# Two small tiles allocated elsewhere in a fused S4D and MLP kernel, so that every operand of the first MLP layer begins at the same place modulo 256 bytes

## The chip, the cores and the metric

The kernel runs on one core of a Trainium2 chip. The metric is the device time of one launch in microseconds (us). Times of engines come from one profiled execution, in which every instruction has a start and a duration. The engines are named as the profile names them: PE (TensorE, matmuls), PEld (TensorE's weight loads, which run beside its matmuls), DVE (VectorE), ACT (ScalarE), POOL (GpSimd) and SP (SyncE, which issues DMAs here).

## The reference

The input is `u`, 2048 tokens of 576 channels, in float32. It is normalised over the channels, and goes two ways that are multiplied at the end:

```python
x  = A_u
xn = _layernorm(x)
s  = A(xn)          # S4D: K = 2 Re sum_n C_n exp(A_n dt t); a causal convolution of each channel
                    # over 2048 tokens, by FFT of length 4096; + xn * D_skip
g  = silu(B(xn))    # MLP: gelu(layernorm(xn) @ w1 + b1) @ w2 + b2, 576 -> 4608 -> 576
out = x + s * g
```

## The kernel before

**The MLP sets the frame.** Tokens come in four blocks of 512 (two halves of the program, with `tb` = 0 and 1 in each), the 4608 hidden units in 12 groups of 384 = 3 x 128. One *slot* is one group for one block of 512 tokens; there are 4 x 12 = 48 slots. Each float32 operand is split into a high part and a low part of the type fp32r, and a product is made of three: high by high, high by low, low by high.

- Layer 1 (`layer1`, line 501; the first slot has its own version, `first_layer1`, line 515) makes three 128 x 512 results in a slot, each by 14 matmuls: four channel blocks of 128 three times, and two matmuls for the last 64 channels, which stand with their low parts in one tile of 128 rows. The stationary operand (loaded as weights) is a 128 x 128 piece of `w1h`, `w1l`, `w1r` or `w1s`; the moving operand is 512 columns of `XH`, `XL` or `XR`. In all there are 48 x 3 x 14 = 2016 of these matmuls.
- After each result `hidden` (line 537) has ACT make the gelu (`h32`) and its high part `hh`, and DVE the low part `hl`.
- Layer 2 (`layer2`, line 554) takes pieces of `hh` and `hl` as weights and 288 columns of `w2h` or `w2l` as the moving operand. The 576 output channels are two halves, `dh` = 0 and 1. Its last four calls of a slot are 9 matmuls each, all of one half: token block 2 with `dh` = 0, then `dh` = 1, then token block 3 with both. There are 3456 matmuls of this form. DVE adds each result to `acc`.

**The S4D part is laid between.** Tables of phases and magnitudes (DVE and ACT, tiles `w`, `mg`, `U`, `v`), the kernel K from them (`kgen`), and a two-stage FFT in matmuls of 32 rows or columns on the tile `A2`. Which of its steps stands where is decided when the program is built: the class `Order` keeps an estimated time for each engine and traces each step when its inputs are due, and pins the order. The order on each engine is thus fixed in the built program.

**Before all that** the prologue runs 22 matmuls on zeros (`warm_up`, line 1133; moving operand and weights are both the last block of `XL`), normalises the first four row blocks, splits the first `w1`, and transposes.

**Tiles.** A tile that is given out once takes the next free bytes of each SBUF partition, in the order of the calls `sb.tile`. So a tile's address follows from what was allocated ahead of it; a start is rounded up to 32 bytes or more. The tile `dsk` (576 bytes a partition, the skip weights) is allocated on line 399, after `XR`; the tile `st` (48 bytes, statistics of a norm) is allocated inside `stats` (line 365), so at its first call `na[0][0](0)` on line 1138, just ahead of `w1_tiles()`.

Of the kernel before, what the change touches and what calls it, by code (L numbers as in the profile page):

```python
# [9 lines left out]
F32 = mybir.dt.float32  # L10
# [7 lines left out]
L, D, N, F = 2048, 576, 128, 4608  # L18
P = 128
# [192 lines left out]
def mixer_kernel(ctx, tc, u, log_a_real, a_imag, c_real, c_imag, log_dt, d_skip, w1, b1, w2, b2,  # L212
                 f1, f2, g2, g1, tvals, ident, out, parts=("mlp", "s4d")):
    nc = tc.nc
    sb = ctx.enter_context(tc.tile_pool(name="sb", bufs=1))
# [13 lines left out]
    def tok(t, b, p0=0, n=P):  # L229
        return dram(t, (b + 16 * p0) * D, [[16 * D, n], [1, D]])  # L230
# [24 lines left out]
    tv, small = tvs[:, :NV], tvs[:, NV:]  # L255
    b1t = sb.tile([P, F // P], F32, name="b1t")
    halfpi, epst = small[:, 0:2], small[:, 2:4]
    w1s = sb.tile([P, G * P], F32R, name="w1s")

    def load_tv():  # L260
# [53 lines left out]
    nc.vector.memset(epst[:, 0:1], EPS)  # L314
    nc.vector.memset(epst[:, 1:2], EPS * EPS)
    nc.vector.memset(w1s[64:].bitcast(F32), 0.0)


    YT, XT = {}, {}
# [28 lines left out]
    def norms(b0, n):  # L348

        def stats(t, part=None):
            if part == 1:
                pass
            elif t == 0 and b0 in (1, 3):
                MV[b0] = SECOND.pop()
            elif t == 0:
                a, r = (UV[:, D + 8 * b0 + 8 * k:D + 8 * b0 + 8 * k + 8] for k in range(2))
                a, r = a.rearrange("p (t k) -> p t k", k=2), r.rearrange("p (k t) -> p k t", k=2)
                MV[b0] = a[:, :n], r[:, :, :n]  # L360
                if n == 1:
                    SECOND.append((a[:, 1:2], r[:, :, 1:2]))
                    PAIR[b0 + 1] = r[:, :, :2]
            if part != 1:
                MV["st"] = sb.tile([P, 2, 6], F32, name="st")
            st = MV["st"]
            for i in range(2) if part is None else (part,):
                nc.vector.bn_stats(st[:, i], XT[b0 + t][:, i * 288:(i + 1) * 288])
            if part != 0:
                nc.vector.bn_aggr(MV[b0][0][:, t], st)  # L370

        def roots():
            mv, rs = MV[b0]
            nc.scalar.activation(rs[:, 0], mv[:, :, 1], AF.Sqrt, bias=epst[:, 0:1], scale=1.0)
            nc.scalar.activation(rs[:, 1], mv[:, :, 1], AF.Sqrt, bias=epst[:, 1:2], scale=1.0 + EPS)

        def recip():
            nc.vector.reciprocal(MV[b0][1], MV[b0][1])

        def second(t):  # L380
            mv, rs = MV[b0]
            y = sb.tile([P, D], F32, name="row", bufs=NROW)
            nc.vector.tensor_scalar(y, XT[b0 + t], mv[:, t, 0:1], rs[:, 1, t:t + 1], op0=OP.subtract, op1=OP.mult)
            if b0 >= 8:
                nc.sync.dma_start(y_s[b0 + t - 8], y)
            else:
                YT[b0 + t] = y

        def first(t):
            mv, rs = MV[b0]  # L390
            x = XT.pop(b0 + t)
            nc.gpsimd.tensor_scalar(x, x, mv[:, t, 0:1], rs[:, 0, t:t + 1], op0=OP.subtract, op1=OP.mult)
            nc.gpsimd.dma_start(tok(xn_s, b0 + t), x)
        return stats, roots, recip, second, first
# [1 line left out]
    XH = sb.tile([P, KB, 2, TB], F32R, name="XH")  # L396
    XL = sb.tile([P, KB, 2, TB], F32R, name="XL")
    XR = sb.tile([P, 2, TB], F32R, name="XR")
    dsk = sb.tile([P, D // 4], F32, name="dsk")
    nc.vector.memset(dsk, 0.0)  # L400

    def y_load(b):
        y = sb.tile([P, D], F32, name="row", bufs=NROW)
# [59 lines left out]
    def w1_tiles():  # L463
        W[1] = (sb.tile([P, KB, G * P], F32R, name="w1h"), sb.tile([P, KB, G * P], F32R, name="w1l"),
                sb.tile([P, G * P], F32R, name="w1r"), w1s)
# [667 lines left out]
    def warm_up(n):  # L1133
        for _ in range(n):
            nc.tensor.matmul(qb[:, 0], zero[:, :P], zero, start=True, stop=True)
    warm_up(22)
    na = [norms(b, 1) for b in range(4)]
    na[0][0](0)
    w1_tiles()

    nc.gpsimd.tensor_copy(small[:, 4:5], MV[0][0][:, 0, 0:1])
    nc.gpsimd.dma_start(idp, dram(ident, 0, [[P, 64], [64 * P, 2], [1, P]]))
# [381 lines left out]
```

## Time and profile before

| | before |
|---|---|
| median of 3 runs | 1108.05 us (1106.91 to 1109.93) |
| the profiled execution, its own time | 1107.08 us |
| its span, first to last instruction | 1105.3 us |
| granted TensorE clock, mean | 0.999 |
| PE busy | 1088.8 us, 99% |
| PEld busy | 941.5 us, 85% |
| DVE busy | 940.9 us, 85% |
| ACT busy | 657.1 us, 59% |
| POOL busy | 197.9 us, 18% |

How it is read: a matmul's duration in a row is its way through the array, near 390 ns for 512 columns, and the next one begins long before it ends. So the pace of a stream of matmuls is read from start to start, not from durations. In the view of instructions in order of time a row has the start, the time from that start to the end of the last instruction in the row, the engine, the line, and behind an x how many instructions the row holds. A matmul's weights are loaded while the matmul before it runs.

### The profile page before, as it was taken

The numbers are of one execution on the slowest core, as the hardware profiler recorded it, in microseconds if no ns is written. First come the engines' busy times: TensorE is split into PE (matmuls) and PEld (weight loads), VectorE is DVE, ScalarE is ACT, GpSimd is POOL, SyncE is SP. The second block draws the span as 40 slices with busy tenths as digits, with TensorE's granted clock in tenths as the row PEclk, the third lists the DMA queues.
The fourth block names the chain that finished last, engine by engine and source line by source line (L and its number), as shares of the span: only waits on it lengthen the run. The fifth ranks groups of instructions, "written<-read, shape, count | busy, mean of one in ns | idle before, by whom it ended". The sixth has DMA issues, their size and how long they took to land.

```text
span 1105.3 us, 27245 instructions
## 1 busy us (share of the span) xinstructions
PE 1088.8 (99%) x11547; PEld 941.5 (85%) x11547; DVE 940.9 (85%) x1510; ACT 657.1 (59%) x977; POOL 197.9 (18%) x282
## 2 busy tenths in 40 slices
PE   9999999999999999999999999999999999999997
PEld 7889989888888888888888888888888888888896
DVE  7799698978999999989699998999999976666466
ACT  6666688666656556657866755665764733233333
POOL 5584532011000200010100001000100021110231
PEclk9999999999999999999999999999999999999999
DMA  8645557333233231633322322233412455342254
GB/s 244 224 147 182 192 205 209 103 107 114 65 87 83 72 93 40 140 94 99 106 85 89 69 77 78 67 98 49 125 22 95 109 139 179 87 127 83 60 186 114
DMA packets 111513, 125.54 MB, mean 114 GB/s; under 512 B 59940, under 2 KB 82032, under 8 KB 110368
## 3 DMA queue, kind: packets, MB, share of 16 engines
q1 hardware_dynamic: 95728, 76.44, 24.7%
q0 software_dynamic: 15104, 46.49, 13.6%
q8 instruction: 90, 1.47, 0.5%
q10 hardware_dynamic: 560, 0.89, 0.3%
q14 instruction: 31, 0.25, 0.1%
HBM read 95.52 MB, written 34.01 MB: 117 GB/s over the span
## 4 chain that ended last, share of the span: by engine, by line
PE 84%; DVE 11%; ACT 2%; issue 2%; DMA 1%; SPq 0%; DVEq 0%; ACTq 0%
PE mxb L569 19%; PE mxa L569 19%; PE mxa L512 19%; PE mxb L512 16%; PE cv L889 3%; PE cv L1000 3%; PE cv L1053 2%; PE cv L962 2%; DVE hl L551 1%; DVE w2l L489 1%; DVE acc L577 1%; PE cv L1080 1%; DVE mg L832 1%; DVE A L949 1%; DVE w L807 1%
## 5 line engine op out<-in xcount | busy, mean ns | idle before, releaser
L569 PE MATMUL mxa<-w2h,hl 128*128 128x288 f32 x573 | 170.0, 297 | 4.0 <-DVE hl L551 4.0
L569 PE MATMUL mxb<-w2h,hh 128*128 128x288 f32 x576 | 171.6, 298 | 0.0
L569 PE MATMUL mxa<-w2h,hh 128*128 128x288 f32 x573 | 171.0, 298 | 0.3 <-DVE acc L577 0.3
L569 PE MATMUL mxb<-w2h,hl 128*128 128x288 f32 x576 | 170.2, 296 | 0.0
L569 PE MATMUL mxb<-w2l,hh 128*128 128x288 f32 x576 | 169.5, 294 | 0.0
L569 PE MATMUL mxa<-w2l,hh 128*128 128x288 f32 x573 | 168.6, 294 | 0.0
L551 DVE TENSOR_TENSOR hl<-h,hh 128x512 fp32r<-128x512 f32 x144 | 98.7, 687 | 73.4 <-ACT hh L548 72.9
L789 POOL DMA_DIRECT2D par<-par_s x36 | 27.4, 761 | 533.0 <-DVE mg L832 520.1
L545 ACT ACTIVATE h<-mxa,b1t 128x512 f32<-128x512 f32 x73 | 50.0, 687 | 117.0 <-PE mxa L512 115.1
L569 PEld LDWEIGHTS mxb<-w2h,hh 128*128 128x128 f32 x576 | 108.1, 188 | 8.6 <-issue 2.9
L569 PEld LDWEIGHTS mxa<-w2h,hh 128*128 128x128 f32 x573 | 107.5, 188 | 7.9 <-issue 2.3
L569 PEld LDWEIGHTS mxa<-w2h,hl 128*128 128x128 f32 x573 | 107.6, 188 | 5.6 <-DVE hl L551 5.6
L569 PEld LDWEIGHTS mxb<-w2l,hh 128*128 128x128 f32 x576 | 108.2, 188 | 0.8
L569 PEld LDWEIGHTS mxa<-w2l,hh 128*128 128x128 f32 x573 | 107.7, 188 | 0.8
L569 PEld LDWEIGHTS mxb<-w2h,hl 128*128 128x128 f32 x576 | 108.1, 188 | 0.0
L545 ACT ACTIVATE h<-mxb,b1t 128x512 f32<-128x512 f32 x71 | 48.9, 688 | 91.3 <-PE mxb L512 90.3
L548 ACT ACTIVATE hh<-h 128x512 fp32r<-128x512 f32 x144 | 90.8, 631 | 4.2
L492 ACT ACTIVATE w2h<-raw 128x576 fp32r<-128x576 f32 x72 | 44.5, 675 | 63.2 <-PE mxa L569 63.1
L577 DVE TENSOR_TENSOR acc<-mxb,acc 128x576 f32<-128x576 f32 x88 | 65.8, 748 | 17.5 <-PE mxb L569 17.3
L512 PE MATMUL mxa<-XH,w1h 128*128 128x512 f32 x284 | 79.3, 400 | 0.5 <-DVE acc L577 0.5
L512 PE MATMUL mxb<-XH,w1h 128*128 128x512 f32 x280 | 78.7, 402 | 0.5 <-ACT h L545 0.5
L577 DVE TENSOR_TENSOR acc<-mxa,acc 128x576 f32<-128x576 f32 x88 | 65.4, 743 | 15.9 <-PE mxa L569 15.5
(235 smaller groups left out, 2483.6 us busy)
## 6 DMA issues: line engine op xcount, KB each, us to landing
raw<-in_B_w_dram SPq DMA_DIRECT2D x72, 288.0 KB, 3.2
raw<-in_B_w_dram SPq DMA_DIRECT2D x96, 192.0 KB, 2.9
par_s<-A POOLq DMA_DIRECT2D x8, 1080.0 KB, 4.8
par<-par_s POOLq DMA_DIRECT2D x36, 240.0 KB, 3.3
f2t<-f2q SPq DMA_DIRECT2D x24, 256.0 KB, 3.4
raw<-in_B_w_dram SPq DMA_DIRECT2D x48, 96.0 KB, 3.3
u_s<-in_A_u_dram POOLq DMA_DIRECT2D x16, 288.0 KB, 4.4
xc<-xn_s SPq DMA_DIRECT2D x48, 96.0 KB, 3.9
```

The source lines that it names most:

```text
L492: nc.scalar.activation(h, r, AF.Copy)
L512: nc.tensor.matmul(q, a, b, start=j == 0, stop=j == len(ops) - 1)
L545: nc.scalar.activation(t, q, AF.Gelu_apprx_tanh, bias=b1t[:, g * G + i:g * G + i + 1], scale=1.0)
L548: LAST[0] = nc.scalar.activation(hh[:, i], t, AF.Copy)
L551: nc.vector.tensor_sub(hl[:, i], t, hh[:, i].bitcast(F32))
L569: nc.tensor.matmul(q[:, dh, :288], a[:, i, c], b[:, i, d], start=i == 0 and k == 0, stop=i == G - 1 and k == 2)
L577: nc.vector.tensor_add(o, q[:, dh:dh + n, :288], b if g == 0 else o)
L789: nc.gpsimd.dma_start(PAR[b].rearrange("p (g i) k -> p g (i k)", g=4), dram(par_s, (b // 6 * CH + b % 6 * 4) * NPAR, [[D * NPAR, P], [24 * ...
L889: nc.tensor.matmul(q[32 * g:32 * g + 32, i // 2, i % 2 * 64:i % 2 * 64 + 64], U[:, ri, 4 * g + i, :], v[:, ri, 4 * g + i, :], start=ri == ...
L962: nc.tensor.matmul(Q1ST[i, x][g // 2][64 * f:64 * f + 64, g % 2].rearrange(order), f1t[r].rearrange("p s k -> p (s k)"), rhs(r, f), start= ...
L1000: nc.tensor.matmul(Q[i][32 * q:32 * q + 32, f, 2 * ri:2 * ri + 2], m[r, 4 * i + q, 32 * ri:32 * ri + 32], A2[r, 4 * p + 2 * i + q // 2, :, ...
L1053: nc.tensor.matmul(QI[q // 2][64 * f:64 * f + 64, q % 2, i], MAT["g2t", p + i // 2][r, i % 2, ri], YS[p + i // 2][0][r, i % 2, ri, f], sta ...
```

## The change

Three lines move. `dsk` is allocated ahead of `w1s`, its clearing stands with the other clearings of the prologue, and `w1_tiles()`, which only allocates, is called ahead of the first `stats`.

```diff
     b1t = sb.tile([P, F // P], F32, name="b1t")
     halfpi, epst = small[:, 0:2], small[:, 2:4]
+    dsk = sb.tile([P, D // 4], F32, name="dsk")
     w1s = sb.tile([P, G * P], F32R, name="w1s")
...
     nc.vector.memset(w1s[64:].bitcast(F32), 0.0)
+    nc.vector.memset(dsk, 0.0)
...
     XR = sb.tile([P, 2, TB], F32R, name="XR")
-    dsk = sb.tile([P, D // 4], F32, name="dsk")
-    nc.vector.memset(dsk, 0.0)
...
     na = [norms(b, 1) for b in range(4)]
+    w1_tiles()
     na[0][0](0)
-    w1_tiles()
```

In the built program every engine has the same instructions in the same order, with the same waits and the same semaphores. What differs is where tiles lie. Bytes from the start of a partition, and the rest modulo 256:

| tile | before | after |
|---|---|---|
| `XH`, `XL`, `XR` (moving, layer 1) | 74944, 91328, 107712: 192 | 75520, 91904, 108288: 0 |
| `w1h`, `w1l`, `w1r` (weights, layer 1) | 120128, 126272, 132416: 64 | 120064, 126208, 132352: 0 |
| `w1s` (weights, layer 1) | 26304: 192 | 26880: 0 |
| `A2`, `acc`, `U` | 27840, 52416, 70848: 192 | 28416, 52992, 71424: 0 |
| `dsk` | 111808: 192 | 26304: 192 |
| `st` | 120064: 0 | 133888: 0 |
| `raw` | 112384: 0 | the same |
| `h32`, `w2h`, `w2l`, `hh`, `hl`, `v`, `f2t`, `kt`, `xc` | 64 | the same |
| `bias2`, `f1t`, `g1t`, `idp` | 128 | the same |

The pieces that a matmul of layer 1 takes begin whole multiples of 512 bytes into their tiles, so they have the rest of the tile. In layer 2 the weights begin at 64; the moving pieces are 2304 = 9 x 256 bytes apart by hidden block and 1152 = 4.5 x 256 bytes by half, so that `dh` = 0 begins at 64 and `dh` = 1 at 192.

## The prediction

> **What bounds the kernel now.** I read the first part of the page, then its chain of work that ended last, then PE's waits, and then the instructions in order of time, since only there a pace can be read.
>
> ```profile
> span 1105.3 us, 27245 instructions
> PE 1088.8 (99%) x11547; PEld 941.5 (85%) x11547; DVE 940.9 (85%) x1510; ACT 657.1 (59%) x977; POOL 197.9 (18%) x282
> PE 84%; DVE 11%; ACT 2%; issue 2%; DMA 1%; SPq 0%; DVEq 0%; ACTq 0%
> ```
>
> PE is busy for 99% of the span, and 84% of the chain is PE itself (the third line), another 2% its own issue. The longest waits of its matmuls say the same:
>
> ```profile
> PE mxa L569 <- DVE hl L551: 4.0, 7, 1.2
> PE mxa L1135 <- POOL XL L1129: 1.3, 1, 1.3
> PE cv L1053 <- issue: 1.2, 1, 1.2
> ```
>
> Four microseconds in seven waits is the most that any one cause costs. So the time is the number of matmuls times their pace, and a change of pace is a change of time, but for the 13% of the chain that DVE and ACT hold. How near DVE is shows in a view by stretches (length; then busy time of PE, PEld, DVE, ACT and POOL, with the number of instructions in brackets; then clock, DMA share, GB/s):
>
> ```profile
> 35.00:300.00 265.00, 264.16 (x2100) 232.45 (x2099) 230.40 (x354) 183.65 (x246) 87.52 (x113) 1.00 0.47 152
> 600.00:900.00 300.00, 296.13 (x3918) 253.28 (x3917) 283.58 (x444) 187.97 (x275) 22.63 (x36) 1.00 0.32 82
> ```
>
> From 600 to 900 us DVE works 283.58 of 300 us: there it can follow a faster PE by some 5%, no more. The clock is 1.00 in both, so no throttle is in play.
>
> **The change, part by part.** It adds, removes and reorders no instruction and no wait, on any engine or queue; only addresses differ. Each term is therefore a price of an address.
>
> *Layer 1, 2016 matmuls.* First the pace now. Three rows, each the first four matmuls of a result of 14:
>
> ```profile
> 100.43 1.10 PE L512 MATMUL mxa<-XH,w1h 128*128 128x512 f32 x4
> 103.69 1.09 PE L512 MATMUL mxb<-XH,w1h 128*128 128x512 f32 x4
> 106.93 0.30 PE L569 MATMUL mxa<-w2h,hh 128*128 128x288 f32 x1
> ```
>
> From 100.43 to 106.93 us two results pass: 6.50 us for 28 matmuls, 232.1 ns each. Moving operand and weights begin at 192 and 64 modulo 256 there, 128 apart. The same form also runs in the prologue, on the last block of `XL` as moving operand and as weights, so at one place. Two windows that end together:
>
> ```profile
> 6.51 2.43 PE L1135 MATMUL mxa<-XL 128*128 128x512 f32 x10
> 7.88 1.07 PE L1135 MATMUL mxa<-XL 128*128 128x512 f32 x4
> ```
>
> Ten take 2.43 us and the last four of them 1.07: six matmuls in 1.36 us, 226.7 ns each. The weights are loaded anew for each of these too. So 5.4 ns a matmul lie between the two streams, 2.4%, and place is one of the things in which they differ (the others: zeros as data, no accumulation, DVE and ACT nearly idle).
>
> Layer 2 gives a second look. Nine matmuls with `dh` = 0 (64 and 64, the same place), nine with `dh` = 1 (192 and 64, 128 apart), and both again, one after the other without a wait:
>
> ```profile
> 111.70 0.30 PE L569 MATMUL mxa<-w2h,hh 128*128 128x288 f32 x1
> 112.88 0.29 PE L569 MATMUL mxa<-w2h,hh 128*128 128x288 f32 x1
> 114.08 0.29 PE L569 MATMUL mxb<-w2h,hh 128*128 128x288 f32 x1
> 115.26 0.29 PE L569 MATMUL mxb<-w2h,hh 128*128 128x288 f32 x1
> 116.46 1.08 PE L512 MATMUL mxa<-XH,w1h 128*128 128x512 f32 x4
> ```
>
> The runs at one place take 1.18 us each, the others 1.20: 131.1 against 133.3 ns a matmul, 2.2 ns less, of which the rounding of four starts leaves about 0.6 uncertain. Data, accumulation and neighbours are alike in these, so place does matter to the pace, and the same place is the better one.
>
> Between 2.2 and 5.4 ns I take the upper. In layer 2 the stream is broken up: a matmul reads 1152 bytes, 4.5 times 256, so the next one starts half a step off from where this one ended. In layer 1 and in the prologue it reads 2048 bytes, eight whole steps, and the distance between the two reads is the same at each of 2016 matmuls. If two reads that keep their distance miss each other once, they go on missing each other, as the prologue's six do. The prologue is the nearer row by form and by bytes.
>
> The sum: 2016 x 5.4 ns = 10.9 us. One matmul in 14 already loads weights at its own place now (`XR` runs while `w1s` is loaded, both 192): x 13/14 = 10.1 us. The 13% of the chain that DVE and ACT hold don't shorten, and some 2% goes to waits that come out where PE arrives earlier at `hl`: x 0.85 = 8.6 us.
>
> *The small matmuls.* Their moving or stationary operands `U` and `A2` move by 64 against partners that stay.
>
> ```profile
> L889 PE MATMUL cv<-v,U 128*32 128x64 f32 x2304 | 39.6, 221 | 0.0
> L1000 PE MATMUL cv<-A,f2t 64*32 64x192 f32 x1536 | 38.7, 332 | 0.2 <-DVE pr L1021 0.2
> L1080 PE MATMUL cv<-A,g1t 64*32 64x384 f32 x192 | 9.6, 505 | 0.0
> ```
>
> 87.9 us together. No row shows how place acts on them; with layer 1's 2.4% in either direction it is +-2.1 us. I take 0, since each reads pieces of several places already.
>
> *DVE and ACT.* Do they care where `acc` lies?
>
> ```profile
> L577 DVE TENSOR_TENSOR acc<-mxb,acc 128x576 f32<-128x576 f32 x88 | 65.8, 748 | 17.5 <-PE mxb L569 17.3
> L577 DVE TENSOR_TENSOR acc<-mxb,bias 128x576 f32<-128x576 f32 x8 | 6.0, 749 | 0.3 <-issue 0.2
> ```
>
> `acc` is read at 192 and `bias` at 128: 748 and 749 ns. I take 0. The clearing of `dsk` keeps its place among DVE's first instructions: 0.
>
> *DMA.* Rows of `acc` and `A2` are written and read at 0 in place of 192. The chain holds one such transfer, the first:
>
> ```profile
> 0.74 3.49 DMA acc<-in_A_u_dram
> 20.93 6.27 DMA kt<-in_A_log_A_real_dram
> ```
>
> `kt` stays. At most a tenth of 3.49 us could go or come, 0.3; the others lie beside PE. I take 0.
>
> Total: -8.6 us, from the profiled execution's 1107.08 us to 1098.5. It stands 0.97 below the median, which gives 1099.5 us for the median to be measured.
>
> **The rivals.** *Only what layer 2 shows.* 2.2 ns in place of 5.4, or 1.6 with the rounding: 2016 x 1.6 to 2.2 x 0.93 x 0.85 = 2.5 to 3.5 us, 1104.5 to 1105.5. For it: the only comparison with real data on both sides. Against it: those streams are broken up as told above.
>
> *Nothing.* The prologue's pace may come from zeros, or from not adding to PSUM, and the 2.2 ns from the order of the operands. Then the time is 1108, +-2.1 for the small matmuls. The Trainium skill, TensorE: Matmul & The Clock Gate, section "Step-by-step: what each phase is for", speaks for this one: the array has two SBUF read ports, and "Loading the next tile's weights doesn't steal SBUF read bandwidth from the running matmul." By that no start address could matter, and the time would stay at 1108. The trace does not bear it out: 131.1 and 133.3 ns stand side by side in one stream that differs in nothing else that I can see.
>
> *Slower: the reads meet at every step.* A constant distance cuts both ways. If the two reads collide at the start of a matmul, they may collide in all 2016, where they now wander through good and bad phases. A bad phase shows in the first layer 1:
>
> ```profile
> 19.51 0.64 PE L527 MATMUL mxb<-XH,w1h 128*128 128x512 f32 x2
> 19.99 0.39 PE L527 MATMUL mxb<-XL,w1h 128*128 128x512 f32 x1
> ```
>
> Two matmuls there take 0.48 us, 240 ns each. At 240 throughout it is 2016 x 7.9 ns = 15.9 us, all of it on the path: 1124. It decides for slower by over 0.3% (3.3 us, about what a measurement of this kernel can tell from no change) where the mean passes 232.1 + 1.6 = 233.7 ns.
>
> **How the numbers follow.** The prologue's pace in layer 1: 0.42, 1097 to 1102.5. Layer 2's gain: 0.27. Nothing: 0.18. Slower: 0.13, of which 0.11 beyond 0.3%. Faster by over 0.3% means under 1104.7: all of the first and half of the second, 0.56. Slower 0.11, and the rest, 0.33, is within 0.3%. The predicted time is that of the first, 1099.5. The range goes from 1097, where the 15% that I took off come back in part, up to 1109, to hold the second and nearly all of the third; it leaves out the slower case and a little at the lower end.
>
> **What would show it.** Right: in the profile after, two results of layer 1 between starts of the same kind as above take 28 x 226.7 = 6.35 us, not 6.50; runs of nine in layer 2 stay at 1.18 and 1.20; DVE's share of the span rises by about 1% of itself. If layer 1 takes 6.43 to 6.46, the second case holds, at 6.50 the third, above 6.55 the fourth. The forecast would be wrong, though layer 1 were faster, if PE's waits for `hl` and `acc` grew from 4 us to ten or more: then DVE holds the time from 300 to 900 us.

## The result, and the profile after

The changed kernel takes 1100.94 us (median of 5 runs) against 1108.05 us: a ratio of 0.9939 with a 95% interval of 0.9925 to 0.9952, 7.1 us less. A second comparison of the same kernel gave 1101.2 us (1100.35 to 1102.47) against 1107.77 us beside it, 0.9942 (0.9929 to 0.9954). One execution of the changed kernel, the one profiled along with the first comparison, ran at a granted clock of 0.65 and took 1505.71 us, so the profile shown here as "after" is that of the second comparison; its own time is 1101.54 us.

First its page, the span, the engines and the chain's shares:

```profile
span 1099.8 us, 27245 instructions
PE 1080.8 (98%) x11547; PEld 940.3 (86%) x11547; DVE 940.7 (86%) x1510; ACT 657.2 (60%) x977; POOL 198.1 (18%) x282
PE 84%; DVE 11%; ACT 2%; issue 2%; DMA 1%; SPq 0%; DVEq 0%; ACTq 0%
```

The instruction counts are those of before, and so are the busy times of DVE, ACT and POOL within 0.2 us. PE lost 8.0 us and PEld 1.2. The instructions in order of time, at the place where two results of layer 1 were shown before:

```profile
100.35 1.07 PE L512 MATMUL mxa<-XH,w1h 128*128 128x512 f32 x4
103.53 1.07 PE L512 MATMUL mxb<-XH,w1h 128*128 128x512 f32 x4
106.70 0.29 PE L569 MATMUL mxa<-w2h,hh 128*128 128x288 f32 x1
```

From 100.35 to 106.70 us are 6.35 us for 28 matmuls, 226.8 ns each, where it was 6.50. Behind it, the runs of nine in layer 2, with `dh` = 0, 1, 0, 1:

```profile
111.47 0.29 PE L569 MATMUL mxa<-w2h,hh 128*128 128x288 f32 x1
112.65 0.29 PE L569 MATMUL mxa<-w2h,hh 128*128 128x288 f32 x1
113.85 0.29 PE L569 MATMUL mxb<-w2h,hh 128*128 128x288 f32 x1
115.03 0.29 PE L569 MATMUL mxb<-w2h,hh 128*128 128x288 f32 x1
116.22 1.09 PE L512 MATMUL mxa<-XH,w1h 128*128 128x512 f32 x4
```

They take 1.18, 1.20, 1.18 and 1.19 us: nothing moved there beyond the rounding. So the gain is a pace, in the one form whose addresses were changed. It is not all kept, as PE's longest waits show:

```profile
PE mxa L569 <- DVE hl L551: 4.9, 7, 1.2
PE cv L1053 <- issue: 1.8, 2, 1.4
PE mxa L1135 <- POOL XL L1129: 1.3, 1, 1.3
```

The wait for `hl` is 0.9 us longer than before, the one at line 1053 is 0.6 longer. To see where all of the span went I added up the distances from one matmul's start to the next one's over both traces. A distance above 260 ns in layer 1, or 165 ns in layer 2, is taken as holding a wait, and what it has above the usual pace stands apart:

| part of the span, us | before | after | difference |
|---|---|---|---|
| layer 1, 2016 matmuls at their pace | 467.9 | 459.6 | -8.3 |
| layer 1, waits | 9.0 | 9.2 | +0.2 |
| layer 2 at its pace | 457.7 | 457.3 | -0.4 |
| layer 2, waits | 14.9 | 17.2 | +2.3 |
| all other matmuls, with their waits | 147.0 | 147.7 | +0.7 |
| ahead of the first, behind the last | 8.8 | 8.8 | 0 |
| span | 1105.3 | 1099.8 | -5.5 |

The count gives the same for other traces of this case: the waits in layer 2 are 14.5 and 14.6 us in the two kernels below whose layer 1 is not faster, and 17.3 us in the one whose layer 1 is faster too. So the 2.3 us are not chance of one execution; a faster layer 1 brings them.

The span's 5.5 us is for two single executions, of which the one before lies 0.97 us below its median (1107.08 against 1108.05) and the one after 0.34 above (1101.54 against 1101.2); with these it is 6.8.

### The profile page after: what moved, and what is told of

Read it like the earlier page. It is cut to its first block, busy times and chain, and to the rows that moved or that the text cites. A ratio compares the mean times of both kernels' runs of the same rounds, so it can differ in the third digit from the quotient of the medians.

```text
span 1503.9 us, 27245 instructions
## 1 busy us (share of the span) xinstructions
PE 1493.8 (99%) x11547; PEld 1169.8 (78%) x11547; DVE 960.1 (64%) x1510; ACT 657.9 (44%) x977; POOL 195.1 (13%) x282
## 4 chain that ended last, share of the span: by engine, by line
PE 99%; DVE 0%; DMA 0%; issue 0%; ACT 0%; ACTq 0%
PE mxa L512 22%; PE mxb L512 22%; PE mxb L569 21%; PE mxa L569 21%; PE cv L889 3%; PE cv L1000 3%; PE cv L962 2%; PE cv L1053 2%; PE cv L1080 1%; PE cv L417 1%; PE mxa L527 0%; DMA acc<-in_A_u_dram 0%; DVE st L370 0%; PE mxa L531 0%; PE mxb L527 0%
## 5 line engine op out<-in xcount | busy, mean ns | idle before, releaser
L569 PE MATMUL mxb<-w2h,hh 128*128 128x288 f32 x576 | 210.7, 366 | 0.0
L569 PE MATMUL mxa<-w2h,hh 128*128 128x288 f32 x573 | 210.1, 367 | 0.0
L569 PE MATMUL mxb<-w2h,hl 128*128 128x288 f32 x576 | 209.5, 364 | 0.0
L569 PE MATMUL mxb<-w2l,hh 128*128 128x288 f32 x576 | 208.5, 362 | 0.0
L569 PE MATMUL mxa<-w2l,hh 128*128 128x288 f32 x573 | 208.0, 363 | 0.0
L569 PE MATMUL mxa<-w2h,hl 128*128 128x288 f32 x573 | 207.8, 363 | 0.0
L512 PE MATMUL mxa<-XH,w1h 128*128 128x512 f32 x284 | 106.2, 510 | 0.0
L512 PE MATMUL mxa<-XL,w1h 128*128 128x512 f32 x284 | 105.9, 506 | 0.0
L512 PE MATMUL mxa<-XH,w1l 128*128 128x512 f32 x284 | 105.6, 505 | 0.0
L512 PE MATMUL mxb<-XH,w1h 128*128 128x512 f32 x280 | 105.0, 510 | 0.0
```

The source lines that it names most:

```text
L512: nc.tensor.matmul(q, a, b, start=j == 0, stop=j == len(ops) - 1)
L569: nc.tensor.matmul(q[:, dh, :288], a[:, i, c], b[:, i, d], start=i == 0 and k == 0, stop=i == G - 1 and k == 2)
```

## The experiments

### One operand moved alone

If the gain comes from the two operands beginning at the same place, moving one alone must not bring it; if it comes from `acc`, `A2` and `U` having left 192, moving `dsk` alone brings it. From the changed kernel, `dsk` alone kept in its new place:

```diff
     na = [norms(b, 1) for b in range(4)]
-    w1_tiles()
     na[0][0](0)
+    w1_tiles()
```

> Only dsk moves: the moving operands of layer 1 begin at 0 modulo 256, its weights stay at 64, 64 apart in place of 128. Theory of the same place: no gain from layer 1, two results 6.45 to 6.55 us, 1106.5 to 1110 us. Rival (what counts is that the moving operand begins at a multiple of 256): 6.35 us and 1101 us. Rival (the gain is from A2, U and acc, which move here too): 1101 us with layer 1 at 6.50 us.

And from the kernel before, `w1_tiles()` alone moved:

```diff
     na = [norms(b, 1) for b in range(4)]
-    na[0][0](0)
     w1_tiles()
+    na[0][0](0)
```

> Only w1_tiles moves: the weights of layer 1 begin at 0, the moving operands stay at 192, 64 apart the other way round. Theory of the same place: 6.45 to 6.55 us for two results, 1106.5 to 1110 us. Rival (the weights' own start counts): 6.35 us and 1101 us.

In the first one the moving operands begin at 0 and the weights at 64, in the second at 192 and 256, which is 0. Measured: 1108.81 us, ratio 1.0012 (1.0003 to 1.0021), and 1109.03 us, ratio 1.0015 (1.0006 to 1.0023). The words "the other way round" in the second expectation are a slip of mine: in both the weights begin 64 bytes behind the moving operand, and both should read alike. They do. The instructions in order of time of the first:

```profile
100.52 1.09 PE L512 MATMUL mxa<-XH,w1h 128*128 128x512 f32 x4
103.78 1.10 PE L512 MATMUL mxb<-XH,w1h 128*128 128x512 f32 x4
107.05 0.29 PE L569 MATMUL mxa<-w2h,hh 128*128 128x288 f32 x1
```

and of the second:

```profile
100.51 1.09 PE L512 MATMUL mxa<-XH,w1h 128*128 128x512 f32 x4
103.77 1.09 PE L512 MATMUL mxb<-XH,w1h 128*128 128x512 f32 x4
107.04 0.30 PE L569 MATMUL mxa<-w2h,hh 128*128 128x288 f32 x1
```

Both take 6.53 us for the 28 matmuls. Over the whole traces the mean from start to start, waits left out, is 233.2 ns in both, against 232.1 before and 228.0 after. Neither half of the change does anything good by itself. And with `A2`, `U` and `acc` at 0 as in the changed kernel, the first of the two has 146.9 us in "all other matmuls" against 147.0 before: the place of these three is worth nothing that shows, neither there nor in the time.

### Both at 64 in place of 0

Is it the equal place, or the place 0? From the kernel before, a tile of 128 bytes is allocated further on, so that `XH`, `XL`, `XR` begin at 64, where the weights already are; `w1s` follows to 64 as well:

```diff
-    g1t = sb.tile([P, 32], F32, name="g1t")
...
     XR = sb.tile([P, 2, TB], F32R, name="XR")
+    g1t = sb.tile([P, 32], F32, name="g1t")
```

> The kernel before, with g1t (128 bytes) allocated behind XR: moving operands of layer 1 and w1s begin at 64 modulo 256, as the other weights do. Same place, but not 0; modulo 512 they are 256 apart. Theory of the same place modulo 256: 6.35 to 6.40 us for two results, 1100 to 1103 us. Rival (starts must be 0 modulo 256): 6.50 us, 1108 us. Rival (the same place modulo 512 is needed): between the two, as the dh = 0 runs of layer 2: 2.2 ns a matmul less than before, 1104 to 1106 us.

Measured: 1102.3 us, ratio 0.9955 (0.9942 to 0.9969), an interval that overlaps the changed kernel's.

```profile
100.60 1.07 PE L512 MATMUL mxa<-XH,w1h 128*128 128x512 f32 x4
103.77 1.07 PE L512 MATMUL mxb<-XH,w1h 128*128 128x512 f32 x4
106.94 0.29 PE L569 MATMUL mxa<-w2h,hh 128*128 128x288 f32 x1
```

6.34 us for 28, and 227.9 ns over the whole trace. So the equal place counts, not the place 0. `XH` and `w1h` are an odd multiple of 256 bytes apart here, so 256 is the step that counts, not 512. (All starts tried in this case are multiples of 64; finer ones were not run.)

### The pace by distance, alone

Two runs in the middle of the kernel can't tell a distance from the data, the neighbours or the accumulation. In the prologue there is less beside PE: from 17.6 us on, where the third of the sequences below begins, DVE, ACT and POOL are idle and the DMA engines all but idle (0.01 of their time or less). There I added seven times 20 matmuls on zeros behind the warm-up, with 512 columns and a weight load for each, whose weights begin 0, 64, 128, 192, 256, 384 and 512 bytes behind the moving operand. The added work makes the program longer (1131.05 us in one execution).

```diff
     warm_up(22)
+    for o in (0, 16, 32, 48, 64, 96, 128):   # floats
+        for _ in range(20):
+            nc.tensor.matmul(qb[:, 0], zero[:, o:o + P], zero, start=True, stop=True)
```

(In the kernel the loop over `o` is written out, a line for each distance.)

> The changed kernel with 7 x 20 more matmuls in the prologue, on the same zeros, 512 columns, weights loaded anew each time, no accumulation; the weights begin 0, 64, 128, 192, 256, 384 and 512 bytes behind the moving operand. The kernel's own work is unaltered; its time is longer by 140 x 0.23 = some 32 us and says nothing. Theory of the same place modulo 256: 226.7 ns a matmul at distances 0, 256 and 512; 232 at 128 and 384; 233 at 64 and 192. Rival (the prologue's 226.7 ns come from zeros or from not accumulating): 226.7 at all seven.

The instructions in order of time, one row for each distance:

```profile
8.38 4.70 PE L1138 MATMUL mxa<-XL 128*128 128x512 f32 x20
12.91 4.83 PE L1140 MATMUL mxa<-XL 128*128 128x512 f32 x20
17.57 4.82 PE L1142 MATMUL mxa<-XL 128*128 128x512 f32 x20
22.23 4.75 PE L1144 MATMUL mxa<-XL 128*128 128x512 f32 x20
26.82 4.71 PE L1146 MATMUL mxa<-XL 128*128 128x512 f32 x20
31.37 4.81 PE L1148 MATMUL mxa<-XL 128*128 128x512 f32 x20
36.02 4.70 PE L1150 MATMUL mxa<-XL 128*128 128x512 f32 x20
40.56 0.60 PE L417 MATMUL cv<-idp,row 128*128 128x128 f32 x4
```

From row to row, divided by 20: 226.5, 233.0, 233.0, 229.5, 227.5, 232.5 and 227.0 ns. The single starts, which the trace also holds, show what is behind these (ns from one start to the next; the lower three are the stretch around 100 us in the kernels):

```
distance   0   227 227 226 227 227 226 ...              steady from the first
distance  64   236 231 235 231 236 231 ...              two in turn, 233
distance 128   230 233 240 233 231 231 229 230 232 241  a cycle of seven, 232
distance 192   236 229 232 226 229 232 226 ...          a cycle of three, 229
distance 256   228 233 231 226 227 227 226 227 ...      steady after three or four
before         241 232 231 232 228 230 233 240 233 231  (128 apart)
dsk alone      231 226 236 231 236 230 236 231 236      (64 apart)
after          226 227 227 226 227 227 226 227 227 226  (0 apart)
```

On zeros and without accumulation, the distances 0, 64 and 128 have the very patterns that they have in the kernel on real data. Neighbours don't set it either: the first sequence ran while DVE was busy for 4.20 of 4.50 us and the DMA engines all the time, the last one with all of them idle, and both settle at 226.7 ns. That the first one is steady from its first matmul is owed to the warm-up ahead of it, which had settled at the same distance. So the step of the prediction that could have been wrong by the prologue's zeros is right, and the rival that rested on them falls. The distance repeats every 256 bytes (256 and 512 like 0, 384 like 128) and is not symmetric: 64 costs 6.5 ns by the rows, 192, which is 64 the other way, 3.0, where the expectation had 233 ns for both.

### Layer 2 in halves of other widths

Layer 2 reads 288 columns, and its runs at one place are only 1.5 ns a matmul faster than those 128 bytes apart. If whole multiples of 256 bytes are what a stream needs to settle, halves of 320 and 256 columns (1280 and 1024 bytes), with all else left as in the changed kernel, should settle too.

```diff
-            d = slice(dh * 288, dh * 288 + 288)
+            d = slice(0, 320) if dh == 0 else slice(320, D)
+            o = q[:, 0, 192:] if dh == 0 else q[:, 1, :256]
...
-                nc.tensor.matmul(q[:, dh, :288], a[:, i, c], b[:, i, d], start=i == 0 and k == 0,
+                nc.tensor.matmul(o, a[:, i, c], b[:, i, d], start=i == 0 and k == 0,
...
-                        st = finish(b, dh * 288, (dh + k) * 288, slot == NSLOT - 1, slot == NSLOT - 1 and j > 1)
+                        st = finish(b, dh * 320, 320 if dh + k == 1 else D, slot == NSLOT - 1, slot == NSLOT - 1 and j > 1)
```

(Not shown: the addition to `acc` in `layer2`, whose slices are written anew for the new halves.)

> The changed kernel, with layer 2's output halves of 320 and 256 columns in place of 288 and 288 (the results lie side by side in PSUM, so the adds stay as they are). The second half now begins 1280 = 5 x 256 bytes into a row: all of layer 2 has moving operands and weights at one place, and every stream is whole steps of 256 bytes long. Theory of the same place: the 576 columns of a pair take 2 x 127.5 to 129 ns in place of 131.6 + 133.1, 7 to 10 ns for each of 1728 pairs, 12 to 17 us, of which some 80% shows: 1087 to 1092 us. Rival (layer 2's 131.6 ns at dh = 0 is what the same place gives there): 1728 x 1.5 ns = 2.6 us, 1098.5 us. Rival (DVE, or 256 columns too short to hide a weight load, takes it back): 1101 us or more.

Measured: 1103.41 us, ratio 0.9961 (0.9946 to 0.9976), so 2.2 us above the 1101.2 us of the changed kernel, and not the gain that was expected. The interval still touches the changed kernel's (0.9929 to 0.9954), so the trace has to tell. The runs of nine in its layer 2, in order of time:

```profile
111.53 0.31 PE L570 MATMUL mxa<-w2h,hh 128*128 128x320 f32 x1
...
112.85 0.28 PE L570 MATMUL mxa<-w2h,hh 128*128 128x256 f32 x1
...
113.93 0.31 PE L570 MATMUL mxb<-w2h,hh 128*128 128x320 f32 x1
...
115.25 0.28 PE L570 MATMUL mxb<-w2h,hh 128*128 128x256 f32 x1
```

1.32 us and 1.08 us for nine, 146.7 and 120.0 ns. The streams do settle, at a pace that is no better: a pair takes 266.2 ns over the whole trace against 264.7 with 288 columns. 1.5 ns for 1728 pairs are 2.6 us, about the loss. The time is in the range of the third case of the expectation, but not for its reason that DVE takes the gain back: the waits in layer 2 are 16.9 us, against 17.2 in the changed kernel. I had scaled the settled pace with the number of columns, and that is wrong.

### The pace by length, alone

What does the settled pace depend on? Again in the prologue (1127.96 us in one execution), 20 matmuls of a kind: 288 columns at distances 0, 64, 128, 192 and 256, then 256, 320 and 384 columns at distance 0, then 512 columns with a weight tile of 64 columns.

```diff
     warm_up(22)
+    for n, o, m in ((288, 0, 128), (288, 16, 128), (288, 32, 128), (288, 48, 128), (288, 64, 128),
+                    (256, 0, 128), (320, 0, 128), (384, 0, 128), (512, 0, 64)):
+        for _ in range(20):
+            nc.tensor.matmul(qb[:m, 0, :n], zero[:, o:o + m], zero[:, :n], start=True, stop=True)
```

(Written out in the kernel here too.)

> The changed kernel with nine more sequences of 20 matmuls on zeros in the prologue (its own work unaltered; the time says nothing). First 288 columns with the weights 0, 64, 128, 192 and 256 bytes behind the moving operand; then 256, 320 and 384 columns at distance 0; last 512 columns at distance 0 with only 64 columns of weights. Theory A (a stream at a good distance costs 17/16 of its columns at 2.4 a ns): 127.5, 113.3, 141.7, 170.0 and 226.7 ns. Theory B (it costs its columns and a fixed 32 cycles for each load of 128 weight columns, as split_320_256 has it): 133.3, 120.0, 146.7, 173.3, and 220.0 ns with 64 weight columns. For layer 2: if one of the distances gives 288 columns at 127 to 130 ns, a shift of hh and hl by 64 bytes can gain; if all give 131 to 133, layer 2 has nothing to gain from place.

```profile
8.80 2.79 PE L1138 MATMUL mxa<-XL 128*128 128x288 f32 x20
11.43 2.83 PE L1140 MATMUL mxa<-XL 128*128 128x288 f32 x20
14.10 2.83 PE L1142 MATMUL mxa<-XL 128*128 128x288 f32 x20
16.76 2.81 PE L1144 MATMUL mxa<-XL 128*128 128x288 f32 x20
19.41 2.79 PE L1146 MATMUL mxa<-XL 128*128 128x288 f32 x20
22.04 2.56 PE L1148 MATMUL mxa<-XL 128*128 128x256 f32 x20
24.44 3.10 PE L1150 MATMUL mxa<-XL 128*128 128x320 f32 x20
27.38 3.63 PE L1152 MATMUL mxa<-XL 128*128 128x384 f32 x20
30.84 4.76 PE L1154 MATMUL mxa<-XL 128*64 128x512 f32 x20
```

With 288 columns the distances give 131.5, 133.5, 133.0, 132.5 and 131.5 ns, all within 2 ns: place hardly matters to such a stream, and layer 2 at 131.6 and 133.1 ns has at most 1.5 ns in half of its matmuls to win. From start to start within the rows, 256, 320 and 384 columns settle at 120.0, 146.7 and 173.3 ns; with 226.7 for 512 columns the four lie on one line, 0.417 ns a column and 13.3 ns for each matmul (226.7 - 120.0 = 106.7 for 256 columns; 120.0 - 106.7 = 13.3). 288 columns would be 133.3 on that line, and take 131.6 at distance 0, in a cycle of four (130, 131, 130 and 135 ns) and not at one pace. So theory B of the expectation holds for 256, 320 and 384 columns and A for none of them. The last row, with 64 weight columns, runs in a cycle from 224 to 236 ns with a mean of 230, where B had 220.0. So the 13.3 ns are not simply in proportion to the weights that are loaded; what they are stays open.

### A plan for the new pace

Layer 2's waits took back 2.3 us. The order of the steps was planned with a layer-1 result of 14 x 0.2315 us. Does a plan made for the new pace save the waits? From the changed kernel:

```diff
-    L1 = 14 * 0.2315
+    L1 = 14 * 0.228
```

and the same with 0.230.

> The changed kernel, with the planner's estimate of a layer 1 matmul set from 0.2315 to 0.228 us, its measured pace now; the order of steps on all engines is planned anew. Theory (some of layer 1's gain is lost since the order was made for the slower pace, and PE now comes early to hl): 1098 to 1100.5 us, PE's waits for hl below 4.9 us. Rival (DVE's load from 300 to 900 us sets it, whatever the order): 1100.5 to 1102.5 us.

> As planned_228 with 0.230, half way. If the order matters in a regular way, its time lies between those of the changed kernel and of planned_228; if the two scatter on both sides of 1101 us, a new plan is only another draw.

Measured: 1106.33 us, ratio to the kernel before 0.9985 (0.9973 to 0.9997), and 1111.98 us, 1.0032 (1.0019 to 1.0044). Both are worse than the changed kernel with its old plan. PE's longest waits, with 0.228:

```profile
PE cv L1053 <- issue: 5.7, 4, 1.7
PE mxa L569 <- DVE hl L551: 2.9, 5, 1.0
```

and with 0.230:

```profile
PE mxa L569 <- DVE hl L551: 6.0, 10, 1.4
PE mxa L512 <- DVE acc L577: 4.4, 2, 2.6
```

The waits for `hl` fell in the first (4.9 to 2.9 us), as a better estimate should make them, but waits at line 1053 came in their place (1.8 to 5.7 us), and in the second both `hl` and `acc` got worse. (The execution with 0.228 that was profiled took 1108.77 us, above its median.) By the count of the table above, the plan with 0.228 has 153.6 us in "all other matmuls" (147.7 in the changed kernel), and the one with 0.230 has waits of 15.7 us in layer 1 (9.2) and 22.4 in layer 2 (17.2). So the old constant, off by 1.5%, was no loss here: both new orders brought waits of their own that are larger than what they were to save. Nor does the time follow the constant: with 0.230 it does not lie between the other two, and neither new plan came out below 1101 us. The changed kernel keeps the lowest median of all that were tried.

## Why the prediction was right, point by point

- *PE sets the time, so a pace is a time.* Right: 84% of the chain before and after, and PE's 8.0 us of busy time became 6.6 to 7.1 us of time.
- *Layer 1 takes the prologue's pace.* Right in what sets the pace, the same place modulo 256 bytes. That it comes from two reads which miss each other was only argued, and no run shows it. The list of what else differs between the two streams had one thing wrong: DVE was not nearly idle beside the prologue's ten matmuls, but busy for 2.26 us of the 2.40 from 6.5 to 8.9 us. It did no harm, since DVE turned out not to matter to the pace. The two results at 100 us came out at 6.35 us, as told. The term of the sum was too large all the same: 10.1 us expected, 8.3 measured. The mean of the whole trace is 228.0 ns, not 226.7. That 226.7 is the settled pace to the digit was luck: the lengths of the two rows give 1.36 us for six, their starts 1.37, which would be 228.3 ns; the single starts decide for 226.7. I had read the pace from six matmuls in mid-stream, and a stream has to get there first: at 116 us the first ones behind layer 2 take 236, 232 and 231 ns before the 227s begin. Of the 1931 distances behind a matmul of layer 1 that hold no wait, 1445 are at 226 or 227 ns and 486 have a mean of 231.9; about nine in ten of these are the first matmuls, mostly 3 to 10, of some 80 streams. The mean before, 232.1, was right. So 2016 x (232.1 - 228.0) = 8.3 us. The factor 13/14 was a slip in the working: the 232.1 is a mean over all 14, the one that already stood well among them, and without the factor the step would have said 10.9 us. The slip hid 0.8 us of the 2.6 by which the pace was misjudged.
- *85% of it is kept.* 8.6 us forecast, 6.6 to 7.1 found, 80 to 86% of the 8.3. The loss went where the step said, to PE waiting in layer 2 (+2.3 us in the table), of which the waits for `hl` are 0.9 us by the profile and the rest is spread over many small ones. How much of the 15% is the chain of DVE and ACT, which was to be 13, no run tells apart.
- *The small matmuls, DVE, ACT, DMA: 0.* Right within what can be seen. "All other matmuls" have 147.0, 146.9 (with `dsk` alone moved) and 147.7 us. DVE's addition at line 577 on `acc`, now at 0, takes the same 748 ns:

```profile
L577 DVE TENSOR_TENSOR acc<-mxb,acc 128x576 f32<-128x576 f32 x88 | 65.9, 748 | 17.1 <-PE mxb L569 16.9
L889 PE MATMUL cv<-v,U 128*32 128x64 f32 x2304 | 39.6, 221 | 0.0
```

- *DVE's share rises by about 1% of itself.* Half of that: 940.9 of 1105.3 us before, 940.7 of 1099.8 after, 0.5%. In the stretch from 600 to 900 us, where it stood at 283.58 us, it hardly moved while PE's waits for `hl` grew by 0.9 us and not to ten, so it did not become the bound:

```profile
600.00:900.00 300.00, 295.15 (x3978) 253.66 (x3966) 283.23 (x443) 186.83 (x274) 23.40 (x37) 1.00 0.32 84
```

- *The rival "only what layer 2 shows"* (2.2 ns a matmul) fell: 4.1 ns in the kernel, and up to 6.5 between the best distance and the worst in the prologue. That place counts for less at 288 columns held (at most 2.0 ns from distance to distance). The reason given, that such a stream is broken up by half steps of 256 bytes, is not shown: halves of 320 and 256 columns are whole steps at one place, and a pair of them took 266.2 ns against 264.7. What they would lose at another distance was not run.
- *The rival "nothing"* fell, and with it what it took from the Trainium skill, TensorE: Matmul & The Clock Gate, section "Step-by-step: what each phase is for", by which two read ports keep the weight load out of the matmul's way. Here 226.5 and 233.0 ns stand in one trace, alike but for the place of the weights. Whether and where the two reads meet, the runs don't show.
- *The rival "slower: the reads meet at every step"* did not come at distance 0, but a constant distance that is worse than the one of before exists, 64: there the mean is 233.2 ns, above the 232.1 of before, and it cost 1.0 to 1.3 us (ratios 1.0012 and 1.0015). Its price, 7.9 ns above the pace of before, was seven times the 1.1 ns found: single matmuls take 240 or 241 ns, no stream does.

## What to carry to other kernels

Where PE sets the time and each matmul has its own weights (all of this is for fp32r), look at the start address of the moving operand and of the weights modulo 256 bytes, and read the pace from start to start: a distance other than 0 cost 1% to 3% of the pace at 512 columns here, and a tile's place in the order of allocation is all that sets it. Moving one tile alone can make it worse, so set both. A pace read from a few matmuls in mid-stream is the best case: take off the matmuls behind every wait before multiplying by the count.

## What the runs showed of the hardware that was not expected

- The pace of a stream of 512 columns with fresh weights is a fixed pattern for each distance, at 0, 64 and 128 bytes the same on zeros and on data: steady 226.7 ns at 0, two in turn (233) at 64, a cycle of seven (232) at 128, a cycle of three (229) at 192 bytes. A stream at distance 0 or 256 pulls itself into the steady pattern, mostly within 3 to 10 matmuls behind a wait. Why these distances have these patterns stays open.
- Settled streams cost 13.3 ns a matmul beside 0.417 ns a column, for 256, 320, 384 and 512 columns. The Trainium skill, TensorE: Matmul & The Clock Gate, section "Back-to-back issue gap", gives N/2.4 + 2.5 ns for an isolated gap, which is 215.8 ns at 512 columns as an estimate from that page, and about 131 ns for a matmul in a sustained stream of 512 columns. The section does not name the type. No fp32r stream of 512 columns in this case had a mean under 226 ns, and the measurement decides here.
- Weights of 64 columns in place of 128 made the stream of 512 columns at distance 0 slower (230 ns against 226.7), not faster.
